# A chunked gated attention and two matmul layers: TensorE in written order, state products in pairs of heads

## The chip, the cores and the metric

One core of a Trainium2 chip. The metric is the device time of one execution in microseconds (us). TensorE (PE in the profile, its weight loads PEld), VectorE (DVE), ScalarE (ACT), GpSimd (POOL) and the DMA queue of SyncE (SP) each work through a list of instructions of their own and wait for each other by semaphores. Every DMA of the loops below is issued from SP's one list.

## What is computed

The inputs are q, k, v and o_gate of 4 batches x 8 heads x 768 steps x 40 dimensions, and two gates per head and step. The reference runs a recurrence over the steps, with a state C (40x40) and n (40) per head:

```python
m_new = np.maximum(f_gate[:, :, t] + m, i_gate[:, :, t])
f_stab = np.exp(f_gate[:, :, t] + m - m_new)
i_stab = np.exp(i_gate[:, :, t] - m_new)
C = f_stab * C + i_stab * np.einsum('bhd,bhe->bhde', vt, kt)
n = f_stab * n + i_stab * kt
h_tilde = np.einsum('bhde,bhe->bhd', C, qt)
denom = np.maximum(np.abs(np.einsum('bhd,bhd->bh', n, qt)), 1.0)
y = sigmoid(o_gate) * h_tilde / denom
```

The 3072 rows of 320 numbers that come out go through two layers: `relu(x @ w_in) ** 2 @ w_out` and `elu(x @ w_in) @ w_out`, with w_in of 320x2048 and w_out of 2048x320.

## The kernel before

**Units.** The attention is worked in chunks of 128 steps. A unit u is one chunk of one batch (24 units, `B` = 4 per chunk), a half-unit n = 2u + g is four of its heads. For each half-unit `scores` (L278) makes four 128x128 products of k and q into one PSUM bank, `emit_E` (L270) makes the decay factors from a broadcast row (`mb`, loaded by `mb_load`, masked on POOL by `mask`), and `emit_P` (L288) multiplies the two on DVE. `pv` (L292) then makes, for each head, the product of these weights with v and a column of ones (128x42, "value"), the product of q with the state (128x42, "state product", the lines `pv<-cst,qks` and `pv<-cf,rqk` of the profile), and once per unit, for the chunk's contribution to the state, k transposed times v (40x42, "state sum", `ut<-kvo`). `evac` (L317) brings them together and updates the state `Cf`. `norm` divides, `trans` turns the unit's result by three TensorE transposes, and `x_hi`, `x_lo` split it into two parts for the first layer.

**Numbers in parts.** Products of the layers run on fp32r operands, each number split into a high and a low part: three products in place of one. A matmul on plain float32 operands is two instructions with a weight load each (64 records for 32 products). From half-unit 16 (`NPLAIN`) on q, k and the state are held stacked in three rows of parts (`qk_hi`, `qk_stack`; `c_hi` on ACT, `c_lo` on POOL and `c_move`, two DMAs, for the state), so that one fp32r instruction does for one product.

**The layers.** A tile j is 512 rows, four units. For each layer l, tile j and block m of 128 of the 2048 columns there is a step k: `mm1` (L469, eight matmuls of 512 columns into `h`), `elem` (L488, on ACT and DVE: `r`, `ghi`, `glo`) and `mm2` (L514, into `acc`; eight matmuls of 512 columns in the first layer, twelve of 320 in the second). A first-layer tile is 16 steps, 256 matmuls of 512 columns.

**What runs beside what.** Units 0 to 3 are done ahead of the loop of steps (`m_pe`, `s_pe`, `pv0`, `evac0`). The other 20 run inside the first layer's tiles 0 to 4, tile j making the rows of tile j + 1. Time is counted in turns t; `attn_pre`, `attn_pe`, `attn_post` (L412 to L450) say what a turn does, and a unit takes four of them. In tile 0 the 16 blocks of weights are also loaded and converted from 64-bit floats on ACT and DVE (`w_load` to `w_lo`), and those of the second layer in the last tile of the first and the first of the second.

**Order.** `emit_pe` (L452) writes TensorE's small attention matmuls in between the big ones of `mm1` and `mm2`. Up to `early.close()` (L745) the engines keep the order in which the program is written. In the loop of steps (L765) all engines, TensorE among them, are ordered by the scheduler of the compiler, which goes by a simulated timeline. The products of step k + 1 are written ahead of `mm2(k)` in the first layer, those of step k + 2 in the second:

```python
for e in first(k + (2 if l or last and m == NF - 1 else 1), small[:mid]):
    elem(e)
```

## Time and profile before

| | |
|---|---|
| time, median of 3 runs | 871.31 us (869.62 to 877.52) |
| span of the profiled execution, first to last instruction | 865.3 us |
| PE busy | 850.7 us, 98% |
| DVE, ACT, POOL busy | 64%, 63%, 17% |
| layer 1, tile 0, from its first `mm2` to that of tile 1 | 61.60 us; a later tile 57.39 us |
| layer 0, tile 2, with four units of attention in it | 79.75 us |
| layer 0, tile 5, without attention | 57.81 us |

The profile gives the span and no separate time of its own execution; the median of the runs is 6.0 us above the span, which is taken as what lies around it. PE counts as busy while a matmul is in its pipeline, and the ends of matmuls are modelled. So the busy share can't tell how well TensorE is used: what a group of matmuls costs is read from start to start, from the first of the group to the first of what follows.

### The profile page before, as it was taken

To read this page: it belongs to the slowest core of one execution; us is meant where nothing else is said; L and a number is where in the kernel's file an instruction comes from. 1 tells how busy PE (TensorE), PEld (TensorE's weight loads), DVE (VectorE), ACT (ScalarE), POOL (GpSimd) and SP (SyncE) were. 2 spreads that over 40 slices of the span, in tenths; PEclk is the share of its full clock that TensorE was granted. 3 is DMA by queue.
4 is the path that set the end of the run, shared out by engine and by line. 5 is a ranking of instruction groups with operands and counts; after the bars stand their busy time and mean duration, and the time that the engine had idled before them with its cause. 6 is when DMAs were issued, how large, how long until landed. Compare 5 with 4: busy or idle time off the path is not lost.

```text
span 865.3 us, 13279 instructions
## 1 busy us (share of the span) xinstructions
PE 850.7 (98%) x4791; PEld 731.5 (85%) x4795; DVE 552.2 (64%) x1002; ACT 547.9 (63%) x1043; POOL 144.5 (17%) x211
## 2 busy tenths in 40 slices
PE   9989998999999999999999998999999999999997
PEld 6778887888888888888888887989989899899996
DVE  5879887556555655455444998666566665665554
ACT  5678885666666666667556997564554554644543
POOL 3131231112111211100000002111111111121111
PEclk9999998999999999999999999999999999999999
DMA  8755556323533353344033560020020100000000
GB/s 256 244 180 175 193 174 174 114 82 108 156 99 99 99 150 116 105 120 131 13 116 120 179 203 37 1 80 1 1 79 2 50 31 1 31 1 1 31 1 31
DMA packets 31384, 81.80 MB, mean 95 GB/s; under 512 B 4087, under 2 KB 9175, under 8 KB 31319
## 3 DMA queue, kind: packets, MB, share of 16 engines
q1 hardware_dynamic: 31031, 80.63, 30.2%
q8 instruction: 38, 0.62, 0.3%
q10 hardware_dynamic: 288, 0.33, 0.1%
q14 instruction: 27, 0.22, 0.1%
HBM read 70.48 MB, written 8.73 MB: 92 GB/s over the span
## 4 chain that ended last, share of the span: by engine, by line
PE 90%; DVE 4%; DMA 2%; ACT 2%; issue 2%; POOL 0%; SPq 0%; POOLq 0%; DVEq 0%; ACTq 0%
PE h L484 39%; PE acc L525 38%; PE pv L303 5%; PE s L284 2%; DMA mb<-negm_dr 1%; PE ut L303 1%; PE dps L647 1%; PE ut L375 1%; PE pv L625 1%; DMA kvo<-kvo 1%; DVE ct L120 1%; DVE ct L119 0%; DVE ct L118 0%; PE acc L608 0%; PE h L600 0%
## 5 line engine op out<-in xcount | busy, mean ns | idle before, releaser
L484 PE MATMUL h<-xh,w 128*128 128x512 f32 x1152 | 365.3, 401 | 2.2 <-DVE r L506 2.2
L484 PEld LDWEIGHTS h<-xh,w 128*128 128x128 f32 x1152 | 216.3, 189 | 45.5 <-DVE r L506 3.0
L508 DVE TENSOR_TENSOR glo<-r,ghi 128x512 fp32r<-128x512 f32 x192 | 132.6, 691 | 133.1 <-ACT r L498 69.4
L525 PE MATMUL acc<-w,ghi 128*128 128x320 f32 x768 | 154.5, 309 | 0.6 <-POOL ghi L507 0.6
L484 PE MATMUL h<-xl,w 128*128 128x512 f32 x384 | 152.6, 397 | 0.0
L502 ACT ACTIVATE r<-h 128x512 f32<-128x512 f32 x96 | 57.4, 598 | 142.8 <-PE h L484 100.2
L525 PE MATMUL acc<-ghi,w 128*128 128x512 f32 x480 | 140.2, 402 | 0.0
L525 PEld LDWEIGHTS acc<-w,ghi 128*128 128x128 f32 x768 | 126.3, 188 | 6.6 <-POOL ghi L507 1.1
L507 POOL TENSOR_SCALAR ghi<-r 128x512 fp32r<-128x512 f32 x96 | 61.6, 641 | 357.1 <-DVE r L506 222.7
L505 DVE SCALAR_TENSOR_TENSOR ex<-ex,th 128x512 f32<-128x512 f32 x96 | 68.7, 715 | 59.7 <-ACT ex L504 58.5
L525 PEld LDWEIGHTS acc<-ghi,w 128*128 128x128 f32 x480 | 87.4, 188 | 15.8
L525 PE MATMUL acc<-w,glo 128*128 128x320 f32 x384 | 100.1, 309 | 0.0
L525 PE MATMUL acc<-glo,w 128*128 128x512 f32 x288 | 92.8, 405 | 0.0
L276 ACT ACTIVATE mb<-mb,cols 128x128 f32<-128x128 f32 x160 | 51.9, 398 | 56.2 <-POOL mb L268 56.2
L484 PEld LDWEIGHTS h<-xl,w 128*128 128x128 f32 x384 | 72.8, 190 | 12.2
L496 ACT ACTIVATE r<-h 128x512 f32<-128x512 f32 x96 | 56.4, 588 | 28.5 <-PE h L484 26.5
L268 POOL TENSOR_SCALAR_AFFINE_SELECT mb<-mb 128x512 f32<-128x512 f32 x40 | 31.7, 795 | 241.0 <-DMA mb<-negm_dr 163.5
L506 DVE SCALAR_TENSOR_TENSOR r<-h,ex 128x512 f32<-128x512 f32 x96 | 66.2, 689 | 2.8
L525 PEld LDWEIGHTS acc<-w,glo 128*128 128x128 f32 x384 | 67.6, 188 | 0.2
L497 ACT ACTIVATE ghi<-r 128x512 fp32r<-128x512 f32 x96 | 60.6, 631 | 8.6 <-PE acc L525 6.9
L503 ACT ACTIVATE th<-r 128x512 f32<-128x512 f32 x96 | 60.8, 633 | 2.8
L498 ACT ACTIVATE r<-r 128x512 f32<-128x512 f32 x96 | 60.6, 632 | 1.9
(108 smaller groups left out, 1017.4 us busy)
## 6 DMA issues: line engine op xcount, KB each, us to landing
raw<-wq SPq DMA_DIRECT2D x32, 704.0 KB
rqk<-qk SPq DMA_DIRECT2D x32, 480.0 KB
kvo<-kvo SPq DMA_DIRECT2D x24, 488.0 KB
mb<-negm_dr SPq DMA_DIRECT2D x40, 256.0 KB
y_dr<-y SPq DMA_DIRECT2D x18, 256.0 KB
out<-y SPq DMA_DIRECT2D x22, 160.0 KB
yr<-y_dr SPq DMA_DIRECT2D x12, 256.0 KB
yr<-y_dr SPq DMA_DIRECT2D x24, 128.0 KB
```

The source lines that it names most:

```text
L303: to.append(lambda: pe.matmul(o, lhsT=l_, rhs=r_, start=True, stop=True))
L484: lambda i=i, a=a, b_=b_: pe.matmul(h[:, 0:n], lhsT=a, rhs=b_, start=(i == 0), stop=(i == len(seq) - 1))
L496: act.activation(out=r, in_=h, func=AF.Relu)
L497: act.activation(out=hi, in_=r, func=AF.Square)
L498: act.activation(out=r, in_=r, func=AF.Square)
L502: act.activation(out=r, in_=h, func=AF.Relu, scale=-1.0)
L503: act.activation(out=th, in_=r, func=AF.Tanh, scale=0.5)
L505: dve.scalar_tensor_tensor(out=ex, in0=ex, scalar=1.0, in1=th, op0=ALU.add, op1=ALU.mult)
L506: dve.scalar_tensor_tensor(out=r, in0=h, scalar=0.0, in1=ex, op0=ALU.max, op1=ALU.subtract)
L507: pool_.tensor_scalar(out=hi, in0=r, scalar1=1.0, scalar2=1.0, op0=ALU.mult, op1=ALU.mult)
L508: dve.tensor_tensor(out=lo, in0=r, in1=hi.bitcast(F32), op=ALU.subtract)
L525: ops.append(lambda: pe.matmul(o, lhsT=l_, rhs=r_, start=first and st, stop=last and sp_))
```

## The change

TensorE's list keeps the written order in the whole loop of steps; the other engines are still ordered by the scheduler. `emit_pe` goes: in a step the order is `mm1` of a step ahead, the scores of one half-unit (with the transposes of the unit before), `mm2`, and, in every fourth turn, `values(u)`: one block with the state products of all eight heads, the eight values and the eight state sums. In the state product one stationary tile holds q of two heads (rows 0 to 39 and 64 to 103, zeros between, a new input `qp`), and `Cf` holds the state of even heads in rows 0 to 39 and of odd heads in rows 64 to 103, with zeros elsewhere, so one plain float32 product of 84 columns does for two heads. The split of the state (`c_hi`, `c_lo`, `c_move`, `Cst`) goes. State sums go to PSUM rows 0 to 39 or 64 to 103 by the head's parity. `evac` works once per unit, with four instructions on 40 rows for the state. `mm2` of the first layer puts all products with the high part first. The products written ahead are those of step k + 1 until step 13, then those of step k + 2. Turns are spread anew over tile 0, and the pool of `mb` has four buffers.

```diff
+T0 = 4 * B
+KP = 64 + D
...
-    a3 = pool("a3", bufs=3, stack=ea)
+    a3 = pool("a3", bufs=4, stack=ea)
...
-    decb = [gc.tile([D, B * H], F32, name=f"decb{i}") for i in range(2)]
-    Cst = [gc.tile([3 * D, H * VW], F32R, name=f"cst{b}") for b in range(B)]
-    Cf = [gc.tile([3 * D, H * VW], F32, name=f"cf{b}") for b in range(B)]
+    decb = [gc.tile([128, B * H], F32, name=f"decb{i}") for i in range(2)]
+
+
+
+    Cf = [gc.tile([128, H * VW], F32, name=f"cf{b}") for b in range(B)]
+
+    def state(b, e, p0=0, p1=H // 2):
+        return Cf[b][64 * e:64 * e + D].rearrange("p (q e d) -> p q e d", e=2, d=VW)[:, p0:p1, e, :]
...
+        ps = pat.tile([128, 512], F32, tag="s" if c > 1 else "in", name="gt")
...
+    def qp_load(u):
+        t = a2.tile([128, 4 * L], F32, tag="qp", name="qp")
+        sp.dma_start(out=t, in_=qp[u])
+        qp_t[u] = t
...
-    def pv(n):
-        u, g = divmod(n, 2)
+    def columns(ps, lhsT, rhs, o):
+        pe.matmul(ps[:, o], lhsT=lhsT, rhs=rhs, start=True, stop=True)
+
+    def state_sum(ps, t, h, at):
+        o = 64 * (h % 2)
+        v1 = t[:, DM + h * VW:DM + (h + 1) * VW]
+        pe.matmul(ps[o:o + D, at:at + VW], lhsT=t[:, h * D:(h + 1) * D], rhs=v1, start=True, stop=True)
+
+    def values(u):
+        b = u % B
+        t, q = kvo_t[u], qp_t.pop(u)
+        ps, pi = bank(u, "pv"), bank(u, "in")
+        PV_t[u] = ps, pi
+        for p in range(H // 2):
+            o = slice(2 * p * VW, 2 * (p + 1) * VW)
+            columns(pi, q[0:KP, p * L:(p + 1) * L], Cf[b][0:KP, o], o)
+        for h in range(H):
+            p = mb_t[2 * u + h // 4]
+            columns(ps, p[:, h % 4, :], t[:, DM + h * VW:DM + (h + 1) * VW], slice(h * VW, (h + 1) * VW))
+        mb_t.pop(2 * u), mb_t.pop(2 * u + 1)
+        if keyed(u):
+            for h in range(H):
+                state_sum(ps, t, h, H * VW + (h // 2) * VW)
+
+    def evac(u):
         c, b = divmod(u, B)
...
-    def evac(n):
-        u, g = divmod(n, 2)
...
-    def split(u):
-
...
+        nu = num_t[u] = a2.tile([128, H, VW], F32, tag="num", name="num")
+        ps, pi = PV_t.pop(u)
+        gb = cols[c % 2][:, 64 + b * H:64 + (b + 1) * H].unsqueeze(2).to_broadcast([128, H, VW])
+        dve.tensor_tensor(out=nu, in0=pi[:, 0:H * VW].rearrange("p (h d) -> p h d", h=H), in1=gb, op=ALU.mult)
+        dve.tensor_tensor(out=nu, in0=ps[:, 0:H * VW].rearrange("p (h d) -> p h d", h=H), in1=nu, op=ALU.add)
+        if keyed(u):
+            for e in range(2):
+                r = slice(64 * e, 64 * e + D)
+                db = decb[c % 2][r, b * H:(b + 1) * H].rearrange("p (q e) -> p q e", e=2)[:, :, e]
+                cf = state(b, e)
+                u3 = ps[r, H * VW:H * VW + 4 * VW].rearrange("p (q d) -> p q d", q=4)
+                dve.tensor_tensor(out=cf, in0=cf, in1=db.unsqueeze(2).to_broadcast([D, 4, VW]), op=ALU.mult)
+                dve.tensor_tensor(out=cf, in0=u3, in1=cf, op=ALU.add)
...
+            ps = bank(u, "in")
...
     def attn_pre(t):
-        n, odd = divmod(t, 2)
...
+        u, k = divmod(t, 4)
+        if k == 0:
+            units(u, lambda u: emit_E(2 * u), lambda u: qk_hi(2 * u + 1), lambda u: mask(2 * u + 1))
+            units(u - 1, norm)
+            units(u, lambda u: qk_stack(2 * u + 1))
+            units(u + 1, lambda v: mb_load(2 * v))
+        elif k == 1:
+            units(u, lambda u: emit_E(2 * u + 1), o_tanh, wk_mult)
+            units(u + 1, lambda v: mb_load(2 * v + 1), lambda v: qk_load(2 * v))
+        elif k == 2:
+            units(u + 1, kvo_load, lambda v: qk_load(2 * v + 1), qp_load)
         else:
-            units((n - 4) / 2, x_hi)
-            units((n - 3) / 2, c_hi, c_lo)
-            units((n - 4) / 2, x_lo)
-            hunits(n, emit_E)
-            units((n - 3) / 2, norm)
+            units(u + 1, lambda v: qk_hi(2 * v), lambda v: mask(2 * v), lambda v: qk_stack(2 * v))
+        if k % 2 == 0:
             gate_at(t + 12, gate_store)
-            gate_at(t + 10, gate_put)
-            hunits(n + 2, mb_load)
-            units((n + 1) / 2, kvo_load)
+            for c in range(1, NCH):
+                if t == (16 * c - 8 if c > 1 else 10):
+                    gate_put(c)
...
+    def attn_pe(t):
+        u, k = divmod(t, 4)
+        if k == 0:
+            units(u, lambda u: [f() for f in scores(2 * u)])
+        elif k == 1:
+            units(u - 1, lambda w: [f() for f in trans(w)])
+            units(u, lambda u: [f() for f in scores(2 * u + 1)])
+        for c in range(1, NCH):
+            if t == (16 * c - 9 if c > 1 else 9):
+                for f in gate_cols(c):
+                    f()
+
     def attn_post(t):
-        n, odd = divmod(t, 2)
...
+        u, k = divmod(t, 4)
+        if k == 0:
+            units(u, lambda u: emit_P(2 * u))
+        elif k == 1:
+            units(u - 1, x_hi)
+            units(u, lambda u: emit_P(2 * u + 1))
+            units(u - 1, x_lo)
+        if k % 2:
...
-    def attn_pe(t):
...
-    def emit_pe(big, small):
...
+    def attn_last(t):
+        u, k = divmod(t, 4)
+        if k == 2:
+            units(u, values, evac)
+
+    def turn(t):
+        for f in (attn_pre, attn_pe, attn_post, attn_last):
+            f(t)
...
+            high = [w[:, 384 + x:512 + x] for x in (0, 128, 256)]
+            for dd in range(3):
+                mm(acc[dd], high[dd], hi, first=True)
             for dd in range(2):
-                ds = slice(384 + dd * 128, 512 + dd * 128)
-                dlo = slice(WC + 448 + dd * 128, WC + 576 + dd * 128)
-                mm(acc[dd], w[:, ds], hi, first=True)
-                mm(acc[dd], w[:, dlo], hi)
-                mm(acc[dd], w[:, ds], lo, last=True)
-            mm(acc[2], w[:, 640:768], hi, first=True)
-            mm(acc[2], w[:, 640:768], lo, last=True)
+                mm(acc[dd], w[:, WC + 448 + dd * 128:WC + 576 + dd * 128], hi)
+            for dd in range(3):
+                mm(acc[dd], high[dd], lo, last=True)
...
+            state_sum(ps, t, 4 * g + i, (4 + i // 2) * VW)
...
-        act.activation(out=Cf[u][0:D, 4 * g * VW:4 * (g + 1) * VW], in_=ps[0:D, 4 * VW:8 * VW], func=AF.Copy)
+        for e in range(2):
+            u3 = ps[64 * e:64 * e + D, 4 * VW:6 * VW].rearrange("p (q d) -> p q d", q=2)
+            act.activation(out=state(u, e, 2 * g, 2 * g + 2), in_=u3, func=AF.Copy)
...
+    es.enter_context(tc.manual_schedule(engines={pe.engine}))
...
-            if j == 0:
-                to = T0 + (21 * (m + 1) + NF - 2) // (NF - 1)
-            else:
-                to = 16 * j + 21 + (16 * (m + 1) + NF - 2) // (NF - 1)
-            while k >= 0 and nt < min(TEND, to):
-                ts.append(nt)
-                nt += 1
+            to = 16 * j + m + 22
+            if j == 0 and m < 13:
+                to = T0 + -(-18 * (m + 2) // 14)
+            ts = list(range(nt, min(TEND, to)))
+            nt += len(ts)
...
-        small = attn_pe(ts[-1]) if ts else []
-        mid = 0 if ts and ts[-1] % 2 else (len(small) + 1) // 2
-        for e in first(k + (2 if l or last and m == NF - 1 else 1), small[:mid]):
+        todo = first(k + (1 if k < NF - 2 else 2))
+        for t in ts[-1:]:
+            attn_pe(t)
+        for e in todo:
             elem(e)
...
-            emit_pe(mm2(k), small[mid:])
+            for f in mm2(k):
+                f()
             put(k)
+        for t in ts[-1:]:
+            attn_last(t)
     es.close()
...
+    qp = np.zeros((NU, 128, 4, L), np.float32)
+    for e in range(2):
+        qp[:, 64 * e:64 * e + D] = units_t(inputs["q"]).reshape(NU, D, 4, 2, L)[:, :, :, e]
```

## Rows read from the trace of the kernel before

**Rows 1.** The page's busy times, shares and instructions of each engine.
```profile
PE 850.7 (98%) x4791; PEld 731.5 (85%) x4795; DVE 552.2 (64%) x1002; ACT 547.9 (63%) x1043; POOL 144.5 (17%) x211
```

**Rows 2.** Windows: length, busy of PE, PEld, DVE, ACT, POOL, clock, DMA share, GB/s.
```profile
52.00:95.00 43.00, 42.24 (x257) 36.06 (x255) 37.96 (x78) 39.59 (x88) 8.50 (x9) 1.00 0.50 165
124.00:150.00 26.00, 23.65 (x134) 18.59 (x132) 19.50 (x48) 16.57 (x33) 7.12 (x7) 0.87 0.54 159
231.87:311.62 79.75, 79.75 (x467) 67.12 (x465) 45.63 (x101) 53.10 (x108) 14.38 (x20) 1.00 0.41 118
464.26:522.07 57.81, 57.65 (x255) 47.41 (x254) 51.50 (x73) 54.67 (x91) 0.90 (x1) 1.00 0.47 156
522.07:583.67 61.60, 59.59 (x329) 53.35 (x327) 43.92 (x65) 37.59 (x66) 12.50 (x17) 1.00 0.12 40
583.67:641.06 57.39, 57.39 (x322) 52.14 (x321) 35.73 (x53) 30.80 (x55) 9.88 (x16) 1.00 0.10 32
```

**Rows 3.** Groups by form of PE in 231.87 to 311.62: count, busy us, mean ns.
```profile
L303 PE MATMUL pv<-kvo,mb 128*128 128x42 f32 x64 | 9.2, 263 | 0.0
L303 PE MATMUL pv<-cst,qks 120*128 120x42 f32 x32 | 4.9, 227 | 0.0
L303 PE MATMUL ut<-kvo 128*40 128x42 f32 x64 | 3.8, 206 | 0.0
L375 PE MATMUL ut<-ident,xt 128*128 128x128 f32 x12 | 2.1, 271 | 0.0
```

**Rows 4.** Timeline of PE in tile 0, small matmuls in blocks: start, length, what.
```profile
61.52 0.98 PE L303 MATMUL pv<-cf,rqk 120*128 120x42 f32 x8
62.33 1.07 PE L303 MATMUL pv<-kvo,mb 128*128 128x42 f32 x8
63.22 1.14 PE L284 MATMUL s<-rqk 120*128 120x128 f32 x8
...
66.10 0.94 PE L525 MATMUL acc<-glo,w 128*128 128x512 f32 x3
```

**Rows 5.** Timeline of PE in tile 1, small matmuls one by one between big ones.
```profile
189.03 0.19 PE L303 MATMUL pv<-cst,qks 120*128 120x42 f32 x1
189.06 0.48 PE L484 MATMUL h<-xl,w 128*128 128x512 f32 x1
189.38 0.19 PE L303 MATMUL pv<-cst,qks 120*128 120x42 f32 x1
```

**Rows 6.** Timeline of PE around one whole block of state sums.
```profile
100.68 0.39 PE L484 MATMUL h<-xh,w 128*128 128x512 f32 x1
101.00 0.81 PE L303 MATMUL ut<-kvo 128*40 128x42 f32 x16
101.75 0.96 PE L525 MATMUL acc<-glo,w 128*128 128x512 f32 x3
102.55 1.30 PE L525 MATMUL acc<-ghi,w 128*128 128x512 f32 x5
```

**Rows 7.** Timeline of PE between tile 0 and tile 1.
```profile
139.52 0.33 PE L375 MATMUL ut<-ident,xt 128*128 128x128 f32 x1
141.13 0.59 PE L303 MATMUL pv<-cst,qks 120*128 120x42 f32 x4 [1.28 <-DVE num L327]
...
146.60 0.63 PE L484 MATMUL h<-xh,w 128*128 128x512 f32 x1
147.03 0.63 PE L484 MATMUL h<-xl,w 128*128 128x512 f32 x1
```

**Rows 8.** Groups by form of DVE and POOL over the whole span.
```profile
L327 DVE TENSOR_TENSOR num<-pv,num 128x168 f32<-128x168 f32 x40 | 13.1, 326 | 0.7
L332 DVE TENSOR_TENSOR cf<-cf,decb 40x336 f32<-40x336 f32 x16 | 8.8, 551 | 16.3 <-POOL clo L348 14.9 <-PE pv L303 1.3
L348 POOL TENSOR_TENSOR clo<-cf,cst 40x336 fp32r<-40x336 f32 x16 | 14.9, 930 | 10.4 <-issue 10.4
```

**Rows 9.** Timeline of PE where tile 0 begins.
```profile
55.48 1.16 PE L284 MATMUL s<-rqk 120*128 120x128 f32 x8 [0.70 <-DVE mb L290]
```

More of the change, by code (lines that the diff above doesn't have):

```diff
@@ L34, with body @@
 N0 = 2 * B
-TEND = 4 * (NU - 1) + 9
-T0 = 2 * N0
+TEND = 4 * (NU - 1) + 7
+T0 = 4 * B
+KP = 64 + D
 NEG = -1.0e30
-def body(tc, qk, kvo, gates, wq, ident_in, qkm_in, out):
+def body(tc, qk, qp, kvo, gates, wq, ident_in, qkm_in, out):
     nc = tc.nc
@@ L393, in x_lo, with units @@
         dve.scalar_tensor_tensor(out=xh[:, 2, cs], in0=xh[:, 2, cs].bitcast(F32), scalar=msk, in1=ps[:, 2, :], op0=ALU.mult, op1=ALU.add)
-    def run(fs, x, low, top):
-        if x % 1 == 0 and low <= x < top:
+    def units(x, *fs):
+        if B <= x < NU:
             for f in fs:
-                f(int(x))
-    def units(x, *fs):
-        run(fs, x, B, NU)
-    def hunits(x, *fs):
-        run(fs, x, N0, NHU)
+                f(x)
     def gate_at(x, f):
@@ L440, in attn_post @@
             gate_at(t + 14, gate_exp)
-    def attn_pe(t):
-        n, odd = divmod(t, 2)
-        ops = []
-        if odd:
-            units((n - 3) / 2, lambda u: ops.append(lambda fs=trans(u): [f() for f in fs]))
-            gate_at(t + 11, lambda c: ops.extend(gate_cols(c)))
-            return ops
-        first, main, st = pv(n - 1) if N0 <= n - 1 < NHU else ([], [], [])
-        return first + (scores(n) if N0 <= n < NHU else []) + main + [lambda: [f() for f in st]]
-    def emit_pe(big, small):
-        done = 0
-        for i, f in enumerate(big):
-            f()
-            want = len(small) * (i + 1) // len(big)
-            for x in small[done:want]:
-                x()
-            done = want
-        for x in small[done:]:
-            x()
+    def attn_last(t):
[5 more added lines that the diff above has]
+            f(t)
     G, HB, ACC = {}, {}, {}
@@ L680, in body @@
     gate_exp(0)
-    emit_pe([], gate_cols(0))
+    for f in gate_cols(0):
+        f()
     gate_put(0)
@@ L739, in body @@
     while t < T0:
[L740 to L742 removed]
+        turn(t)
         t += 1
@@ L749, in body, with first @@
         behind.enter_context(tc.issue_after(next(i for i in reversed(nc.cur_bb.bb.instructions) if i.engine == e.engine)))
+    es.enter_context(tc.manual_schedule(engines={pe.engine}))
     nt, nm = T0, 0
-    def first(k, small):
+    def first(k):
         nonlocal nm
@@ L757, in first @@
         while nm <= min(k, len(steps) - 1):
-            emit_pe(mm1(nm), small)
-            small = []
+            for f in mm1(nm):
+                f()
             todo.append(nm)
             nm += 1
-        emit_pe([], small)
         return todo
```

87 lines of the change are left out of this document (8 added, 79 removed).

## Prediction

> **What bounds the kernel now.** I read the page's busy shares first, then the windows by stage, then the groups of one tile, then single stretches of TensorE's timeline. The first says TensorE: 98%, no other engine over 64% [rows 1]. That share alone can't carry the argument, since small matmuls count as busy while they wait in the pipeline. The windows can. Tile 5 of the first layer, with no attention, takes 57.65 us of TensorE for 255 recorded matmuls of 512 columns, 0.226 each; a tile of the second layer takes 57.39; tile 2, with four units of attention, 79.75 with no idle time [rows 2]. So in tiles 1 to 4 the time is the sum of TensorE's instructions, and what a small matmul costs there counts in full. Only three places show anything else. In tile 0, from 52 to 95, ACT is busy for 39.59 of 43 us and DVE for 37.96, beside TensorE. Between tiles 0 and 1 TensorE idles for 2.35 of 26 us and the granted clock falls to a mean of 0.87. Where the second layer starts, a tile takes 61.60, with 2.01 idle [rows 2].
>
> **What attention costs TensorE.** A tile's 256 big matmuls at 0.226 are 57.9 us; 79.75 − 57.9 = 21.9, less some 0.6 for a chunk's five gate matmuls (estimated at 0.12 each, as the small ones below), leaves 21.3 for four units, 5.3 each. A unit has 8 scores, 8 state products, 16 instructions of values and 16 of state sums, and 3 transposes [rows 3].
>
> In a block, eight instructions of values last from 62.33 to 63.22, 0.111 each, and eight plain state products of 42 columns 0.81, 0.101 each [rows 4]. Alone between big ones, a small and a big take 0.35 (189.03 to 189.38), so the small costs 0.35 − 0.226 = 0.124 [rows 5]. The small matmul starts late and the big one 0.03 behind it, so nothing of it is free. A block of 16 state sums costs more than its 0.75 us: the big matmul ahead takes 0.32 in place of 0.226, and the three behind 0.80 in place of 0.68. That is 0.09 + 0.75 + 0.12 = 0.96 [rows 6]. With 35 × 0.124 + 0.96 = 5.3 the tile's figure is met: in tile 2 the small ones cost about what they do alone.
>
> The Trainium skill speaks against the change here: "TensorE: Matmul & The Clock Gate", section "Step-by-step: what each phase is for", has the next weights loaded while the running matmul streams, so a small matmul between big ones should hide its load, and one in a block should not. By it the gathering into blocks loses (last rival); by the rows it gains 0.013 for each.
>
> **The change, part by part.** *Blocks, units 8 to 23.* The count stays: four state products for pairs, two instructions each, are eight as before. 35 × 0.111 + 0.96 = 4.84 against 5.3 is 0.45 a unit; the last four units have no state sums, and the two blocks of four scores may keep an end each, so I take 0.4: 16 × 0.4 = 6.4, rounded down to **−6**. Not shown before is a plain product of 84 columns. From below it is the 0.101 of 42 columns; from above, the scores of 128 columns: 66.10 − 63.22 = 2.88 for eight of them, eight state products and eight of values, less 0.81 and 0.89, is 1.18, 0.148 each [rows 4]. I take 0.111, as 42 columns and 128 differ so little; the upper end costs 8 × 0.037 = 0.3 a unit, 6 us in all.
>
> *Plain units 4 to 7.* There the state products were 16 instructions and become 8: 0.81, with the 0.4 above 1.2 a unit, **−5** for four.
>
> *State sums by parity.* Neighbouring heads write different PSUM rows. Before, all wrote the same, so no row prices it. Below: no change. Above: each costs a full slot of 0.111 in place of 0.96 / 16 = 0.060, 16 × 0.051 × 16 units = 13 us. I take nothing, as the operands keep their sizes. The Trainium skill ("TensorEngine Tiling (Array Packing)", "Key Properties") says that changing the tiling mode drains TensorE, not changing the tile; the 0.32 at the entry of the block fits the first half [rows 6], and no run here shows the second.
>
> *The split state.* 16 instructions each on ACT and POOL (0.93 on POOL [rows 8]) and 32 small DMAs go. They cost TensorE time only where the state is late, between tiles 0 and 1.
>
> *evac.* Before: four of 128x168 at 0.326 at most and two on 40 rows at 0.551 at most, 2.4 a unit [rows 8]. After: two of 128x336, at most twice 0.326 each, and four of 40x168, at most 0.326 each: 2.6. Under it lie 45.63 of 79.75 us of DVE in tile 2, and TensorE reads the state only four units later: nothing. In tile 0 that cover is thin; 0.2 × 4 is less than 1 us and is in the waits below.
>
> *qp.* 128 x 512 numbers, 256 KB a unit, one more DMA in SP's list behind `kvo` and `qk` of the next unit and three turns ahead of its use; DMA engines are busy for 0.41 of tile 2 [rows 2]. Nothing there. Were it late, `values` and everything behind it on TensorE would be.
>
> *Between tiles 0 and 1.* TensorE waited there 1.28 for `num` (139.52 to 141.13), and before 150 big matmuls ran 0.43 apart (146.60 to 147.03), 1.2 GHz in place of 2.4 [rows 7]. The lost clock is 0.13 × 26 = 3.4, with 2.35 idle 5.7 us [rows 2]. Of what fed that stall the splitting of the state goes and `mb` has a fourth buffer; the stacking of q and k that begins there, on ACT and DVE, stays. Bounds 0 and −5.7; I take **−3**.
>
> *Written order.* Now TensorE stops at the first thing that is late, and all behind it stops. From tile 1 on each small group is a step or more behind what it needs: scores wait for the `emit_P` of the turn before, `values` for the `emit_P` of a turn earlier, with at least a group of `mm1` and one of `mm2` (1.8 us each) between, and first-layer products run two steps ahead. No wait. In tile 0, with one step ahead, `mm2(k)` follows `mm1(k)` by `mm2(k−1)`, `mm1(k+1)` and the scores, about 4.5 us, while ACT and DVE are some 90% busy. Where the tile begins, scores wait for `emit_P`: 0.70 already before [rows 9], and now the next `mm1` would be behind them. Bounds: 0, and about 0.9 in each of 16 steps, 14. I take **+3**, near the lower end, as TensorE also has less to do there and the high-part products now come first in `mm2`.
>
> *Second layer.* It had the same step ahead before and no idle time but 2.01 at its start, which DVE sets: 0, at best −2.
>
> Sum: −6 − 5 − 3 + 3 = −11. 865.3 − 11 = 854.3, and with the 6.0 between span and median **860.3 us**; I say 860.
>
> **Rivals.** *Fewer waits.* Written order adds nothing, and the 5.7 and the 2 come back: 865.3 − 6 − 5 − 5.7 − 2 + 6.0 = 853, or a little less. For it: those waits hang on a few late items. Against: DVE is no less loaded.
>
> *Waits in tile 0 eat the gain.* 14 in place of 3: 871. For it: ACT and DVE at 90%. Against: the old list too waited in order once it was written.
>
> *Parity costs a slot.* +13: 873.
>
> *Slower: DVE's backlog stops the value blocks in tile 0.* `values(u)` waits for `emit_P` on DVE behind weight conversions; each time TensorE stands, then runs at half clock, as between the tiles: 1.5 waited and 3.4 of clock, 4.9. Should it happen in units 4 to 8, 24.5: 865.3 − 14 + 24.5 + 6.0 = 882. It begins to decide when `emit_P` is late by more than the 3.6 us of a step. Against: 40 small matmuls from 61.52 to 66.10, as long as such a block, with the clock at 1.00 in that window [rows 2, 4]; only with waits in it did it fall.
>
> *Blocks lose the overlap.* Alone, a small one would cost the 0.03 behind which the big one starts, and in a block 0.111: 32 × 0.08 × 20 = 51 us, some 920. Rows 5 speak against it.
>
> **How the numbers follow.** Forecast 0.48, its own range 853 to 868 (of it 0.36 below 862.6, faster by over 1%, and 0.12 above); fewer waits 0.16, faster; waits eat the gain 0.12 and parity 0.06, within 1%; DVE's backlog 0.16 and lost overlap 0.02, slower. One per cent is about what a measurement of this kernel can tell from no change. So faster 0.36 + 0.16 = 0.52, same 0.12 + 0.12 + 0.06 = 0.30, slower 0.18. The range leaves out the slower cases and the tail of the best: 848 to 877.
>
> **What would show it.** Right: in tile 2 some 78 us, values 0.11 apart in one block, state sums 0.06 or less, no idle time of TensorE from tile 1 on, clock 1.00 between tiles 0 and 1. Wrong: TensorE idle in tile 0 before `s`, `acc` or `pv`, with DVE or ACT as what ended it, or a clock below 1.00 in tile 0; values or state products over 0.12 apart.

## The result, and the profile after

The changed kernel takes 881.9 us (median of 20 executions, 877.1 to 894.4); the kernel before, beside it, 875.4 (20 executions, 869.6 to 882.8). The ratio is 1.0072 [1.0047, 1.0098]: not 11 us faster, but some 6 us slower. TensorE's share is as it was:

```profile
PE 856.6 (97%) x4759; PEld 738.4 (84%) x4763; DVE 555.5 (63%) x994; ACT 540.8 (61%) x1035; POOL 121.1 (14%) x195
```

This line answers [rows 1] and says nothing of the loss. The windows do: of the kernel after, the stretches that answer [rows 2] (length, busy of PE, PEld, DVE, ACT, POOL, granted clock, DMA share, GB/s). First the start of tile 0, then the passage to tile 1, tile 2, tile 5, and the first two tiles of the second layer.

```profile
52.00:95.00 43.00, 29.63 (x135) 23.56 (x134) 34.22 (x65) 31.39 (x71) 9.44 (x12) 0.71 0.46 151
124.00:150.00 26.00, 23.24 (x132) 19.57 (x131) 18.00 (x36) 15.78 (x30) 4.43 (x6) 0.93 0.39 123
250.79:328.65 77.86, 77.86 (x468) 65.84 (x466) 46.66 (x100) 49.77 (x102) 9.75 (x16) 1.00 0.44 128
476.20:534.30 58.10, 58.10 (x257) 47.88 (x256) 50.44 (x71) 55.24 (x91) 0.62 (x1) 1.00 0.50 167
534.30:597.50 63.20, 59.81 (x322) 53.54 (x322) 42.92 (x63) 35.49 (x63) 11.73 (x16) 0.97 0.11 34
597.50:655.00 57.50, 57.50 (x322) 52.12 (x321) 35.42 (x53) 30.77 (x55) 9.91 (x16) 1.00 0.10 31
```

Tile 2 is 79.75 − 77.86 = 1.9 us shorter, as forecast. But from 52 to 95 TensorE did 135 matmuls where it had done 257, was idle for 13.4 us, and had a clock of 0.71 where it had 1.00. Its timeline there (start, length, line, what, count; in brackets the idle time before it and what ended that):

```profile
56.10 0.84 PE L466 MATMUL h<-xh,w 128*128 128x512 f32 x3
64.77 2.08 PE L294 MATMUL s<-rqk 120*128 120x128 f32 x8 [7.83 <-DVE mb L300]
66.50 0.77 PE L466 MATMUL h<-xh,w 128*128 128x512 f32 x1
...
71.09 1.43 PE L507 MATMUL acc<-ghi,w 128*128 128x512 f32 x5 [0.83 <-ACT ghi L479]
76.32 1.65 PE L507 MATMUL acc<-glo,w 128*128 128x512 f32 x3 [3.80 <-DVE glo L490]
```

TensorE stands for 7.83 us ahead of the scores of half-unit 9, which need `emit_P(8)`, then for `ghi` and `glo`. In [rows 9] the same scores had waited 0.70. In all TensorE idles 16.8 us in tile 0; half clock begins inside the two long stops, at 59.9 (to 70.2) and at 73.6 (to 87.2).

**One number to read the times with.** The mean granted clock c of an execution and its span S give its time at half clock (1.2 in place of 2.4 GHz), h = 2 (1 − c) S (not the `h` of the profile's lines, the output of `mm1`). It differs between executions of one program, and the time goes with it: over the 89 executions of the kernel before that all comparisons together hold, h is 7 to 49 us (median 28) and the time is 864.7 + 0.40 h, with 1.0 us of scatter; over the 20 of the kernel after, h is 32 to 73 (median 47) and the time 864.2 + 0.39 h. So by this fit the two kernels are alike at equal clock, and the loss is 0.40 × (47 − 28) = 7.6 us of clock. The profiled execution of before was a rare one: its h is 9, and 3 of the 89 are under 12. The profiled execution of after took 885.95 us for a span of 884.2: what lies around a span is 1.8 us, not 6.0.

In the table below the times and h are medians of all executions of a kernel, while the ratios leave out those more than 1.5% above its fastest.

### The profile page after: what moved, and what is told of

It reads as the page before. It is cut to its first block, busy times and chain, and to the rows that moved or that the text cites. A ratio compares the mean times of both kernels' runs of the same rounds, so it can differ in the third digit from the quotient of the medians.

```text
span 884.2 us, 13302 instructions
## 1 busy us (share of the span) xinstructions
PE 856.6 (97%) x4759; PEld 738.4 (84%) x4763; DVE 555.5 (63%) x994; ACT 540.8 (61%) x1035; POOL 121.1 (14%) x195
## 4 chain that ended last, share of the span: by engine, by line
PE 81%; DVE 5%; DMA 2%; ACT 2%; issue 1%; POOL 0%; SPq 0%; POOLq 0%; DVEq 0%; ACTq 0%
PE h L466 36%; PE acc L507 36%; PE pv L303 3%; PE in L303 2%; PE s L294 2%; DMA mb<-negm_dr 1%; PE in L360 1%; DVE ct L119 1%; PE pv L308 1%; DMA kvo<-kvo 1%; DVE ct L118 1%; DVE w L135 1%; DVE glo L490 1%; DMA yr<-y_dr 0%; ACT mb L286 0%
## 5 line engine op out<-in xcount | busy, mean ns | idle before, releaser
L466 PEld LDWEIGHTS h<-xh,w 128*128 128x128 f32 x1152 | 218.6, 190 | 44.9
L507 PE MATMUL acc<-w,ghi 128*128 128x320 f32 x768 | 170.6, 309 | 0.6 <-POOL ghi L489 0.6
L507 PEld LDWEIGHTS acc<-w,ghi 128*128 128x128 f32 x768 | 132.5, 188 | 8.5 <-POOL ghi L489 0.9
L507 PE MATMUL acc<-ghi,w 128*128 128x512 f32 x480 | 129.8, 398 | 1.8 <-ACT ghi L479 1.5
L507 PE MATMUL acc<-w,glo 128*128 128x320 f32 x384 | 119.4, 311 | 3.6 <-DVE glo L490 3.6
L507 PE MATMUL acc<-glo,w 128*128 128x512 f32 x288 | 82.9, 397 | 6.6 <-DVE glo L490 6.6
L507 PEld LDWEIGHTS acc<-w,glo 128*128 128x128 f32 x384 | 72.3, 188 | 4.4 <-DVE glo L490 4.3
L507 PEld LDWEIGHTS acc<-glo,w 128*128 128x128 f32 x288 | 54.5, 190 | 19.5 <-DVE glo L490 7.9
L278 POOL TENSOR_SCALAR_AFFINE_SELECT mb<-mb 128x512 f32<-128x512 f32 x40 | 28.3, 713 | 269.2 <-DMA mb<-negm_dr 191.7
```

Source lines behind the costliest of these rows:

```text
L466: lambda i=i, a=a, b_=b_: pe.matmul(h[:, 0:n], lhsT=a, rhs=b_, start=(i == 0), stop=(i == len(seq) - 1))
L507: ops.append(lambda: pe.matmul(o, lhsT=l_, rhs=r_, start=first and st, stop=last and sp_))
```

## The experiments

All kernels, with the ratio to the kernel before of the same comparison. "At equal clock" is the median of time − 0.40 h. The changed kernel ran 20 times; a3, b1, c1, c2, c4, d1, d3 and e1 ran four times each, and their medians are good to 1 or 2 us; the others ran ten times.

| kernel | time, us | ratio | h, us | at equal clock |
|---|---|---|---|---|
| before, all comparisons | 875.5 | | 28 | 864.6 |
| after | 881.9 | 1.0072 [1.0047, 1.0098] | 47 | 863.1 |
| a0_before | 874.9 | 1.0014 [0.9972, 1.0055] | 27 | 864.4 |
| a1_serial_ahead | 884.6 | 1.0104 [1.0059, 1.0149] | 49 | 864.3 |
| a2_scheduler | 878.3 | 1.0019 [0.9974, 1.0064] | 49 | 858.4 |
| a3_before_written | 919.0 | 1.0483 [1.0381, 1.0586] | 53 | 897.6 |
| b1_serial_loop | 886.2 | 1.0135 [1.0062, 1.0209] | 51 | 864.5 |
| c1_turn_ahead | 888.6 | 1.0177 [1.0104, 1.0251] | 55 | 866.1 |
| c2_turn_ahead_idle | 887.6 | 1.0165 [1.0098, 1.0232] | 42 | 871.3 |
| c4_turn_ahead_two_steps | 886.8 | 1.0142 [1.0067, 1.0218] | 57 | 862.6 |
| d1_turn_before_weights | 886.0 | 1.0156 [1.0082, 1.0229] | 50 | 866.2 |
| d2_turn_scheduler | 872.1 | 0.9977 [0.9937, 1.0018] | 42 | 855.4 |
| d3_fill_stop | 890.4 | 1.0198 [1.0145, 1.0252] | 52 | 869.9 |
| e1_pace | 889.6 | 1.0155 [1.0085, 1.0226] | 64 | 865.2 |
| e2_pace_two_ahead | 880.4 | 1.0082 [1.0045, 1.0118] | 36 | 866.8 |
| e3_scheduler_pace | 871.2 | 0.9950 [0.9912, 0.9989] | 38 | 855.4 |
| e4_before_changed_pace | 877.2 | 0.9987 [0.9942, 1.0031] | 29 | 865.8 |
| f1_products_ahead_scheduler | 872.1 | 0.9947 [0.9905, 0.9988] | 44 | 856.2 |
| f2_products_ahead | 877.4 | 1.0016 [0.9979, 1.0052] | 36 | 862.0 |

### Which part of the change loses: the order, or the blocks

The kernel before, unchanged (a0_before), is the measure:

> The kernel before, unchanged, to see the granted clock and the span of each of its executions. Theory C (the clock ahead of the loop): the changed kernel loses some 10 us because TensorE runs at half clock from 26 to 53 us, and the kernel before doesn't; then nearly all executions here show a mean clock of 0.99 or more, and the scores of half-unit 8 start near 44 us. Rival: the kernel before falls to half clock there in part of its executions too, and its spread of 869 to 883 us is that; then means between 0.96 and 0.995 are mixed. Ratio 1.000 either way.

874.9 us, and its ten executions have an h of 16 to 42, as the rival said. Its profile has a span of 873.2 and 17.1 us of half clock ahead of the loop, which the profile of before had not. So half clock there is no mark of the change.

a1_serial_ahead takes the alternation of row groups out of the state sums ahead of the loop:

```diff
-        for i in range(4):
+        for i in (0, 2, 1, 3):
             state_sum(ps, t, 4 * g + i, (4 + i // 2) * VW)
```

> The changed kernel, with one edit: the state sums ahead of the loop are written with the two even heads first and the two odd heads behind, so that neighbours no longer alternate between PSUM rows 0 to 39 and 64 to 103. Theory C1 (alternating state sums run two at a time, TensorE gets ahead of DVE, waits for emit_P and falls to half clock): a block of eight takes 0.43 us in place of 0.29, the wait of 0.75 us at 25 us is gone, the clock stays at 1.00 from 26 to 53 us, the scores of half-unit 8 start at 44 to 46 us in place of 54, and the time falls by 7 to 10 us, to 872 to 875. Rival C2 (the fall has another cause, the added qp loads or the ACT copies): block 0.43 us, clock still 0.5 from 26 us, time within 2 us of the changed kernel's 882.

884.6 us, h = 49: no gain. The alternation ahead of the loop doesn't bring the clock down. A stop of 7.35 us stands ahead of the same scores.

a2_scheduler gives TensorE's list in the loop back to the scheduler:

```diff
-    es.enter_context(tc.manual_schedule(engines={pe.engine}))
```

> The changed kernel without the written order of TensorE in the loop of steps: the scheduler orders it, as in the kernel before. Theory W (written order is what costs at the start of tile 0 and at the start of the second layer): the wait of 7.8 us for emit_P before the scores of half-unit 9 and the 3.8 us for glo in the first mm2 are filled with other products, tile 0's first mm2 to tile 1's comes 8 us sooner, and the time falls by 6 to 12 us, to 870 to 876, though the half clock ahead of the loop is still there. Rival (those waits follow from the late start and the half clock, not from the order): within 2 us of 882.

878.3 us, between its two forecasts. At equal clock it is 4.7 us below the changed kernel and 6.2 below the kernel before, but h is 49 again. So the written order costs 4.7 us at equal clock, the rest of the change gains 6.2, and the extra half clock comes without the written order too. A stop is there as well, though the profile doesn't show what ended it (timeline of TensorE):

```profile
61.13 2.05 PE L294 MATMUL s<-rqk 120*128 120x128 f32 x8 [5.17 <-issue]
```

a3_before_written adds that line to the kernel before.

> The kernel before with one edit, TensorE in written order in the loop of steps (its interleaving as written stays). Theory W: waits of 5 us or more where tile 0 begins and some 2 to 3 us where the second layer begins, time up by 6 to 12 us, 881 to 887, with the clock ahead of the loop at 1.00. Rival: within 3 us of the kernel before.

919.0 us, far above both forecasts, 33 more at equal clock, with half clock ahead of the loop too (25.9 to 56.6). TensorE stands for 8.04 us on `ghi` (69.26), 4.94 on `glo` (75.42) and 3.03 on `num` (89.33). A list written for a scheduler isn't one to be run as it stands; in the changed kernel, whose list was made for it, written order costs 4.7 us in place of these 33.

### The state sums

b1_serial_loop orders the state sums of `values` by parity, so that eight in a row write the same PSUM rows:

```diff
-            for h in range(H):
+            for h in (0, 2, 4, 6, 1, 3, 5, 7):
                 state_sum(ps, t, h, H * VW + (h // 2) * VW)
```

> The changed kernel with the state sums of values(u) written even heads first, odd heads behind, so that in the loop neighbours no longer alternate between two ranges of PSUM rows. Theory P (alternating state sums run two at a time): a block of 16 takes 0.75 us from its first to the next big matmul in place of 0.43, and 16 units give 5 us more of TensorE; tiles 2 and 3 are 1.2 us longer each, 79.1 in place of 77.9, and the time at equal clock is 3 to 5 us more. Rival (the pairs in the trace are only how starts are recorded): tiles 2 and 3 stay at 77.8.

One block of the changed kernel, and then the state sums of this one (timelines of TensorE):

```profile
276.76 1.02 PE L303 MATMUL in<-cf,qp 104*128 104x84 f32 x8
277.61 1.92 PE L303 MATMUL pv<-kvo,mb 128*128 128x42 f32 x16
279.46 0.51 PE L308 MATMUL pv<-kvo 128*40 128x42 f32 x16
279.89 0.50 PE L466 MATMUL h<-xh,w 128*128 128x512 f32 x1
```

```profile
273.66 0.69 PE L308 MATMUL pv<-kvo 128*40 128x42 f32 x16
274.28 0.50 PE L466 MATMUL h<-xh,w 128*128 128x512 f32 x1
```

From the first of 16 to the product behind them it is 0.43 us alternating, 0.62 by parity, and 0.75 in [rows 6], where all write the same rows. In the trace of after the 16 start in pairs, at 279.457 and 279.464, 279.516 and 279.523, and so on; in [rows 6] they start one by one, about 0.037 apart. So against the same rows alternation is a gain of 0.32 a unit, 5 us in 16 units. The order by parity gives back 0.19 of it a unit, not the 0.32 that was expected: tiles 1 to 3, each from its first `mm2` to that of the next, are together 1.8 us longer in b1_serial_loop (12 units; 12 × 0.19 is 2.3), so the pairs aren't only a matter of how starts are recorded. As a time, b1_serial_loop is 1.4 us above the changed kernel at equal clock, under the 3 to 5 forecast, and four executions can't tell that from nothing.

### The stop ahead of the scores

c1_turn_ahead puts turn 16 (factors, scores and score product of half-unit 8) ahead of the loop; c2_turn_ahead_idle also doubles the independent products that fill TensorE there; c4_turn_ahead_two_steps also runs the first products of tile 0 two steps ahead:

```diff
-    while t < T0:
+    while t < T0 + 1:
         turn(t)
...
-    nt, nm = T0, 0
+    nt, nm = T0 + 1, 0
```

```diff
-        idle((4, 2, 2, 2, 2, 2, 2, 2, 0, 0)[i])
+        idle((4, 4, 4, 4, 4, 4, 4, 4, 0, 0)[i])
```

```diff
-        todo = first(k + (1 if k < NF - 2 else 2))
+        todo = first(k + 2)
```

> The changed kernel with one turn more ahead of the loop of steps: turn 16 (the factors, scores and emit_P of half-unit 8) is written where all engines still keep the written order, so ACT makes the factors before the next weight conversions and DVE makes emit_P before them too. Theory S (TensorE's stop of 7.8 us before the scores of half-unit 9 is DVE's and ACT's order, and the half clock behind it follows from the stop): the stop falls below 1.5 us, the half clock at 60 to 70 and 74 to 87 us goes or shrinks to under 10 us, tile 0's first mm2 comes at 62 to 65 us where the clock ahead of the loop is as in the changed kernel, and the time is 870 to 876. Rival S2 (the next late thing takes its place, glo of step 0): first mm2 after 69 us, time 879 to 883.

> As the one before, and four instead of two of the filling matmuls of 512 columns per half-unit ahead of the loop. Theory C (the half clock ahead of the loop comes from too little work on TensorE there, by chance of the moment): the mean clock of nearly all executions is over 0.985, the scores of half-unit 8 start at 46 to 48 us, and the time is 5 to 9 us under the one without them, 863 to 869. Rival (the clock falls there whatever stands in the gaps, or the 3 us that 14 more matmuls take eat the gain): no more than 2 us less, or more.

> As c1, and the first-layer products written two steps ahead from the first step on, not from step 14. Theory W1 (one step ahead is too little in tile 0, where ACT and DVE are loaded): the waits of mm2 for glo in tile 0 (3.8, 0.6, 0.6, 0.8 and 2.1 us in the changed kernel) shrink to under 2 us in all, and the time is 3 to 5 us under c1's. Rival (the products ahead then wait for their weights, which are converted one block per step): waits for w before h, time as c1's or above.

888.6, 887.6 and 886.8: none gains. In the first the stop ahead of the scores is still 6.75 us (60.70), the one for `glo` 4.63 (72.82); in the third they are 4.71 (65.10) and 4.67 (77.45). The extra filling takes h from 55 to 42 and costs 5.2 us at equal clock: what it gives, it takes. ScalarE's list shows why the turn helped so little: its factors still stood behind the conversions of the weights (in c1_turn_ahead ScalarE waits 5.72 us for VectorE's conversion, until 56.46, converts until 58.7, and makes eight factors then). First the list of after, then of a0_before (timelines of ScalarE):

```profile
59.94 0.79 ACT L127 ACTIVATE w<-ct 128x704 fp32r<-128x704 f32 x1 [5.63 <-DVE ct L119]
60.63 0.82 ACT L107 ACTIVATE ct<-raw 128x704 f32<-128x704 f32 x1
61.36 0.83 ACT L108 ACTIVATE cu<-raw 128x704 int32<-128x704 uint32 x1
62.10 2.43 ACT L286 ACTIVATE mb<-mb,cols 128x128 f32<-128x128 f32 x8
64.43 0.45 ACT L267 ACTIVATE kvo<-kvo 128x320 f32<-128x320 f32 x1
64.79 0.57 ACT L478 ACTIVATE r<-h 128x512 f32<-128x512 f32 x1
```

```profile
55.13 0.79 ACT L128 ACTIVATE w<-ct 128x704 fp32r<-128x704 f32 x1 [5.40 <-DVE ct L120]
55.83 0.83 ACT L108 ACTIVATE ct<-raw 128x704 f32<-128x704 f32 x1
56.56 0.83 ACT L109 ACTIVATE cu<-raw 128x704 int32<-128x704 uint32 x1
57.29 0.59 ACT L496 ACTIVATE r<-h 128x512 f32<-128x512 f32 x1
57.77 1.27 ACT L276 ACTIVATE mb<-mb,cols 128x128 f32<-128x128 f32 x4
```

Both wait over 5 us for VectorE's conversion of weights. Then before takes the first `r` at once, after only behind eight factors and a tanh, 2.7 us later; and while `r` and the factors are late, TensorE stands.

d1_turn_before_weights writes the turn ahead of those conversions, d2_turn_scheduler does it with the scheduler, and d3_fill_stop leaves the order and fills the stop:

```diff
             x_lo(B - 1)
             idle(2)
+            turn(T0)
+            t = T0 + 1
             w_lo()
```

```diff
+            if u == B:
+                idle(28)
             units(u, lambda u: [f() for f in scores(2 * u + 1)])
```

> The changed kernel with turn 16 (factors, scores and score product of half-unit 8) written in the part ahead of the loop, and there ahead of the last blocks of weight conversions, which kept ScalarE from those factors when the turn stood behind them. Theory A (the loss is TensorE's stops in tile 0, made by the written order, and the half clock that follows them): the 7.8 us stop ahead of the scores of half-unit 9 shrinks below 2 us, the first second product comes before 66 us (71.1 in the changed kernel), the half clock at 60-70 and 74-87 us goes at least in part, the span is near 875 and the time 873 to 879 us. Theory B (the stop is only where another lateness shows, the weight conversions or VectorE's load early on): the stop moves to the conversions' readers, the first products of the tile or their splits, of the same length, and the time stays at 882 or above. Theory C (the loss lies in the blocks): no change, 882.

> The same early turn 16, and the scheduler instead of the written order for TensorE in the loop. Theory A: no written stop in tile 0, and of the two the one with less half clock after 56 us: 868 to 874 us, below the kernel before. Theory B: as the kernel with the scheduler alone, 878 us. Theory C: 878 or above.

> The changed kernel with 28 independent products of 128x512 bf16, that nothing reads, written on TensorE ahead of the scores of half-unit 9, where it stands still for 7.8 us. They take about 6 us at the full clock, so the chain of work isn't longer, but the engine is not still. If the half clock follows from the engine's standing still (theory A), the half clock at 60-70 us goes (5 to 10 us of it), the products behind it run at the full clock, and the time falls by 0.4 times that, to 878-880 us. If the half clock there has another cause, the trace shows it at the same place, and the time is 882 to 886 us.

d1_turn_before_weights: the stop ahead of the scores is gone, and the time is 886.0. The timeline of its TensorE:

```profile
55.66 0.86 PE L466 MATMUL h<-xh,w 128*128 128x512 f32 x3
66.46 2.50 PE L507 MATMUL acc<-ghi,w 128*128 128x512 f32 x5 [9.95 <-ACT ghi L479]
72.58 0.80 PE L507 MATMUL acc<-glo,w 128*128 128x512 f32 x1 [3.61 <-DVE glo L490]
```

The stop moved to the first `mm2`, and grew to 9.95 us. So the theory that the turn's place makes the stop is refuted; the forecast of theory B came true. The timeline of TensorE in d3_fill_stop, with the products that nothing reads, and then two of its windows (columns as above):

```profile
53.71 6.22 PE L630 MATMUL dps<-dr 128*128 128x512 bf16 x28
61.19 1.16 PE L294 MATMUL s<-rqk 120*128 120x128 f32 x8 [1.26 <-DVE mb L300]
...
67.51 1.84 PE L509 MATMUL acc<-ghi,w 128*128 128x512 f32 x5 [3.32 <-ACT ghi L481]
73.15 1.22 PE L509 MATMUL acc<-glo,w 128*128 128x512 f32 x2 [3.81 <-DVE glo L492]
```

```profile
56.00:64.00 8.00, 6.74 (x35) 3.89 (x32) 5.62 (x11) 7.64 (x20) 0.00 (x0) 1.00 0.60 201
72.00:80.00 8.00, 6.85 (x35) 6.48 (x37) 7.81 (x15) 5.84 (x11) 0.00 (x0) 0.50 0.49 158
```

From 56 to 64 the clock is now 1.00 (after: 0.75), so there it had followed from TensorE's standing still. But TensorE stands next at 67.51 and 73.15, half clock comes there, for 17.1 us from 68.3, and the time is 890.4, above what either theory expected: h is no lower (52) and the time at equal clock is 6.8 us higher, so the 6.2 us of filling were not free. d2_turn_scheduler meets its forecast: 872.1 us, and from 56 to 88 TensorE idles 4.6 us in place of 12.5.

### The pace of the turns

One part of the change the prediction had passed over: the changed kernel does two turns (eight factors, a tanh) ahead of step 0, the old one none. e1_pace gives the changed kernel the old pace; e2_pace_two_ahead adds `first(k + 2)`; e3_scheduler_pace is e1_pace with the scheduler; e4_before_changed_pace gives the new pace to the kernel before.

```diff
             if j == 0 and m < 13:
-                to = T0 + -(-18 * (m + 2) // 14)
+                to = min(to, T0 - (-21 * (m + 1) // (NF - 1)))
```

```diff
-                to = T0 + (21 * (m + 1) + NF - 2) // (NF - 1)
+                to = T0 + -(-18 * (m + 2) // 14)
...
-            while k >= 0 and nt < min(TEND, to):
+            while nt < min(TEND, to):
...
+        else:
+            emit_pe([], small[mid:])
```

> The changed kernel with the old pace of tile 0: no attention turn before step 0, then 21 turns in 15 steps. Theory P (the new pace puts two turns, 8 factors and a tanh, ahead of the first relu on ScalarE, and the first square behind 18 factors): the 7.8 us stop ahead of the scores of half-unit 9 goes or falls below 2 us, the first square comes within 6 us of the first relu's input being ready, the first second product before 66 us, half clock after 56 us below 14 us; time 870 to 876 us. Theory Q (the blocks leave TensorE nothing small to run while ScalarE is late, whatever the pace): the stops in tile 0 still sum to over 15 us, time 880 us or more.

> The old pace, and in tile 0 the first products two steps ahead as in the other tiles. Theory P: as with the pace alone, or 2 us less, as the 3.8 us wait for the low part goes too: 868 to 875 us. Theory Q: 880 us or more.

> The old pace and the scheduler for TensorE in the loop. Theory P: the 5.2 us stop at 61 us of the kernel with the scheduler alone goes, half clock falls from some 49 us towards the 28 of the kernel before, and the gain of the blocks is left: 864 to 870 us. Theory Q: 876 to 880 us, the stop stays.

> The kernel before, with the changed kernel's pace of tile 0: two turns before step 0, then 18 in 14 steps. Theory P: a stop of 3 to 6 us at about 58 to 65 us, the first square 3 us later or more, half clock behind it; 878 to 886 us. Theory Q: small state sums and state products fill it, no change: 873 to 877 us.

In both kernels the time is that of theory Q. e1_pace takes 889.6, with 5.43 us of stop at 69.62 and 5.04 at 100.07 on `xt`. e4_before_changed_pace shows no loss, 877.2, although a stop of 2.92 us at 54.98 waits for `r`. The pace alone is not the cause, in either kernel. e2_pace_two_ahead, at 880.4 within its rival's forecast, is 9 us below e1_pace by its clock alone (h = 36 for 64); at equal clock it is 1.6 above. It still stops for 4.74 us on `glo` (67.23) and 5.50 on `xt` (88.56). With the scheduler the old pace alone helps: e3_scheduler_pace takes 871.2 us, 7 below a2_scheduler (3.0 of it at equal clock, the rest h = 38 in place of 49), though TensorE still waits at its start:

```profile
64.60 0.80 PE L466 MATMUL h<-xh,w 128*128 128x512 f32 x1 [4.86 <-ACT r L478]
```

### The first products ahead of the conversions

f1_products_ahead_scheduler (e3_scheduler_pace and this) and f2_products_ahead (e1_pace and this) write the first two products and their element work into the part ahead of the loop, before the weight conversion for which ScalarE waits.

```diff
             w_lo()
+            for k in range(2):
+                for f in mm1(k):
+                    f()
...
             w_bits()
+            if i == N0:
+                elem(0)
+                elem(1)
             w_hi()
...
-    nt, nm = T0, 0
+    nt, nm = T0, 2
```

> Scheduler and old pace, and the first two products, their relu, squares and low parts written in the part ahead of the loop, on ScalarE ahead of the weight conversion that waits some 5 us for VectorE. If the lateness of ScalarE's first relu makes the stop at the loop's start: the 4.9 us stop (64.6 us in the kernel with scheduler and pace) goes or halves, the first second product comes some 8 us earlier in tile 0 (under 12 us after the first first-layer product, against 18.4), half clock in tile 0 below 10 us; 862 to 868 us. If something behind it is as late (weights, VectorE): the stop moves, 870 to 875 us.

> The same with TensorE in written order. If ScalarE's lateness makes the stop: the stop ahead of the scores of half-unit 9 below 3 us, the first second product under 12 us after the first first-layer product (13.5 with the old pace alone), 872 to 880 us, against 889.6 with the old pace alone. If the written order turns any lateness into a stop further on: 882 us or more, with the stops at the low parts and at the transposed units.

In f1_products_ahead_scheduler the first `mm2` comes 6.3 us after the first product (18.4 in e3_scheduler_pace) and TensorE has no stop over 0.4 us until 78.5. Yet the time is 872.1, 856.2 at equal clock: nothing gained. The stop is now where tile 0 ends (timeline of TensorE, and a window around the stop):

```profile
56.79 1.31 PE L507 MATMUL acc<-ghi,w 128*128 128x512 f32 x5
...
148.31 0.90 PE L360 MATMUL in<-ident,xt 128*128 128x128 f32 x3
153.93 1.22 PE L466 MATMUL h<-xh,w 128*128 128x512 f32 x2 [4.71 <-ACT xh L370]
```

```profile
140.00:160.00 20.00, 13.27 (x63) 10.37 (x63) 9.69 (x24) 6.95 (x18) 2.31 (x4) 0.66 0.47 141
```

The first product of tile 1 waits for the rows of unit 7, with a clock of 0.66 in that window. So with the scheduler ScalarE's lateness does set the first stop, and taking that stop away doesn't take the rest of tile 0's waits away.

In the written order the same edit is worth 12 us (877.4 against 889.6) and h falls from 64 to 36; that kernel is level with the kernel before, and its time is within the first forecast. Its trace isn't: the stop ahead of the scores of half-unit 9 is still 5.79 us (72.59), where under 3 was expected, and the first `mm2` comes 12.6 us after the first product. That trace is of its slowest execution (889.3 us, h = 62), so where the median's 12 us were won is not shown.

## Why the prediction was wrong, step by step

**Blocks, state products and values: right in kind, the tile's length by luck.** Eight products of 84 columns take 277.61 − 276.76 = 0.85 us, 0.106 each (0.111 taken), sixteen of values 1.85, 0.116 each (0.111). Tile 2 came to 77.86 ("some 78"), but not for the reasons given: 4 × 0.32 = 1.3 of its 1.9 us are the state sums, and the gathering itself gave 0.6 where 1.6 was taken. The −5 of the plain units in tile 0 can't be told apart from that tile's stops.

**State sums by parity: wrong sign.** Bounds of 0 and +13 left out a gain. It is −5 us by the traces. The prediction quoted the Trainium skill ("TensorEngine Tiling (Array Packing)", section "Key Properties") on the drain when the mode changes and had no row on changing the tile; the same section says that tiles operate independently, and the pairs that start 7 ns apart agree.

**Between tiles 0 and 1: right.** In [rows 7] this passage, from the transposes of unit 7 to tile 1's first products, had a stop and half clock. In the changed kernel it lies later, from 150 to 170, and there TensorE is busy for 20.00 of 20 us at a clock of 1.00 (lines of its timeline, after: the transposes of unit 7, then the state products of unit 8, which wait for nothing).

```profile
151.93 0.49 PE L360 MATMUL in<-ident,xt 128*128 128x128 f32 x3
...
158.18 1.02 PE L303 MATMUL in<-cf,qp 104*128 104x84 f32 x8
```

The stop of 2.09 us and the half clock that the window from 124 to 150 still shows lie earlier, at 131.95 in tile 0.

**The split state, evac, qp: right.** The state's work on VectorE is as costed ([rows 8]: 0.326 each), and nothing waits for `qp`, whose transfers land in 2.6 us (groups of VectorE over the whole span, after: busy, mean ns of one, idle time before):

```profile
L340 DVE TENSOR_TENSOR cf<-pv,cf 40x168 f32<-40x168 f32 x32 | 10.4, 326 | 0.5
L331 DVE TENSOR_TENSOR num<-in,cols 128x336 f32<-128x336 f32 x20 | 10.0, 502 | 2.7 <-PE in L303 2.7
```

**Written order in tile 0, +3 within 0 to 14, with the clock at nothing: the step that failed.** It was priced as up to 0.9 in each step, without the clock. Measured are single stops of 7.83 and 3.80 us at the tile's start, 16.8 in the tile, with half clock in and behind them. The order alone is the smaller part of the miss: taking it away is worth 4.7 us at equal clock, which is inside the bounds. What the sum had no term for is the additional half clock, +7.6 us, and it stays without the written order (h = 49).

The place shows in the traces when the matmuls of `mm1` and `mm2` in the loop are counted from their first to their 257th (256 is a tile of the first layer):

| profile | ahead of the first, us | first to 257th | from there to the end |
|---|---|---|---|
| a0_before | 51.6 | 98.6 | 723.0 |
| a2_scheduler | 52.1 | 108.9 | 716.1 |
| after | 54.9 | 112.0 | 717.3 |

Behind tile 0 the change gains 5.7 us of the 9 forecast for it (blocks and passage). In tile 0 it loses 13.4 where −2 was forecast (plain units and written order), and 10.3 of that is there with the scheduler too. Ahead of it, it loses 3.2, with 27.3 us of half clock for 17.1. (These are single executions, with h = 26, 49 and 58.) The tile was argued from the 90% of ACT and DVE as a load spread evenly; the stop comes where one engine hangs on another for 5 us (ACT on VectorE's conversion) with the factors queued behind.

**Second layer, 0: wrong, small.** Its first tile is 63.20 for 61.60, with two stops on `glo` where [rows 2] had 2.01 of idle time (timeline of TensorE, after):

```profile
536.95 0.42 PE L507 MATMUL acc<-w,glo 128*128 128x320 f32 x1 [2.12 <-DVE glo L490]
...
547.34 0.42 PE L507 MATMUL acc<-w,glo 128*128 128x320 f32 x1 [1.27 <-DVE glo L490]
```

**The base, 865.3 + 6.0: wrong reading.** Of the 6.0 only 1.8 lies around a span; the rest is by how much that execution, with its h of 9, was faster than the median of the three runs. That median itself was 4 us under the 875.4 of twenty executions. So the clock was taken as given, 1.00 outside one place; it is a term of 11 us (0.40 × 28) in the kernel before and 19 in the kernel after.

**The rivals.** The slower one said 882 us, by stops in tile 0 and the half clock behind them, decided when `emit_P` is late by more than a step, 3.6 us. Tile and mechanism came so, and the 7.83 us wait is for `emit_P`. That its 882 meets the measured 881.9 is luck: it set 24.5 us of stops and clock against gains of 14, and measured are 12.3 against 6.2, on a base 4 us higher. Its place was wrong (scores and `mm2`, not the value blocks), and so was the argument against it: small matmuls in [rows 4] show TensorE under the scheduler, which may put other work there.

**The sum in measured terms.** Change without written order −6.2 (a2_scheduler against before, at equal clock; forecast −6 − 5 − 3 = −14), written order +4.7 (forecast +3), clock 0.40 × 19 = +7.6 (forecast nothing): +6.1, measured 881.9 − 875.4 = +6.5.

**What stays open.** Why the new form of the attention has more half clock even with the scheduler (38 to 49 us against 28). In the profiles some of it begins ahead of the loop (stretches of 13.7 to 44 us in the new form; 0, 3, 17 and 31 in the four profiles of the old one). No stop there tells the two apart: in after a wait of 0.75 us at 25.09 stands next to the fall of the clock at 25.8, but e4_before_changed_pace waits 0.71 at 24.85 and keeps the full clock until 41.6. Some lies from tile 0 to the start of tile 1 (13.7 to 31 against 7 to 21). Alternation, the place of a turn, the pace and the first products were each tried; each moves the stops. With the scheduler turn or pace took 7 to 11 us off h; in the written order neither alone did, only the pace together with more products ahead.

## What to carry to other kernels

Here the fixed order was safe where the other engines ran ahead of TensorE (tile 2, no idle time), and dear where they didn't: look for the one stretch in which the helpers hang on each other, and write that stretch's order from their queues, or leave it to the scheduler. Price a stop with the half clock behind it, and before forecasting from one profile, ask how its granted clock stands to that of other executions. A stop that was taken away showed up at the next late item (d1_turn_before_weights, f1_products_ahead_scheduler), as the helpers' work in that stage was what it had been. The version that kept the blocks, gave the order back to the scheduler and kept the old pace is the best found, by little (871.2 us, 0.995 [0.991, 0.999] of the kernel before, with the versions that have the early turn or the first products ahead level with it).

## What the runs showed of the hardware

State sums (40x42) into PSUM that alternate between rows 0 to 39 and rows 64 to 103 start two at a time: 0.43 us for 16, against 0.62 by parity and 0.75 into the same rows. An execution of one program has between 7 and 49 us at half clock (before), with half clock coming ahead of the loop in some profiles and not in others after TensorE has been as busy: from 22 to 30 us it is busy for 7.84 of the 8 us, with 68 matmuls, both in the profile of before and in that of a0_before, at a clock of 1.00, and from 32.0 the clock is 0.50 in a0_before and stays at 1.00 in before. By the fit each microsecond at half clock costs 0.40 us. A TensorE kept busy through a wait by products that nothing reads kept its clock at 1.00 there (0.75 without), and lost it at the next waits, so the filling bought no time.
